# When an attention kernel starts its transposes, and when its planner counts results as ready

## The chip, the cores and the metric

The kernel runs on one core of a Trainium2 chip. The metric is the device time of one execution in microseconds (us). Three executions of the kernel before took 1045.03 us in the median, between 1043.71 and 1046.25 us. Engines are named as in the profile: PE is TensorE's matmul, PEld its weight load, DVE VectorE, ACT ScalarE, POOL GpSimd, SP the queue that issues the DMAs.

## The reference

Two attention blocks (A and B) with a compressive memory work on the same input of 2048 tokens and 640 channels, 32 heads of 20 channels, in four segments of 512 tokens. A gate that depends on the token mixes their results.

```python
logits = einsum("bhqd,bhkd->bhqk", qs, ks) * scale + mask   # mask: only earlier or equal keys
a_dot = einsum("bhqk,bhkd->bhqd", softmax(logits), vs)
a_mem = einsum("bhld,bhde->bhle", phi(qs), M) / (einsum("bhld,bhd->bhl", phi(qs), z)[..., None] + 1e-6)
o = g * a_mem + (1.0 - g) * a_dot          # g = sigmoid(beta), one value a head
M = M + einsum("bhld,bhle->bhde", phi(ks), vs); z = z + phi(ks).sum over tokens
...
out = gate * (o_A @ wo_A) + (1 - gate) * (o_B @ wo_B)    # gate = sigmoid((x * gate_w).sum(-1))
```

q, k and v are x @ wq, x @ wk, x @ wv; phi(t) is t + 1 above zero and exp(t) below.

## The kernel before

**Stages.** A pair of block and segment is called t (0 to 7), a group of four heads a quad, so that there are 64 quads, eight for each t. The large products (projections to q, k, v, and the output projection) are taken in three terms, of high and low parts of both factors, so that each has 15 or, for v, 60 matmuls on each half of the array. For a quad the kernel makes the scores once with queries on the partitions to find each row's maximum (an S unit, L1096; DVE reads the bank at L1114), and a second time with keys on the partitions (a T unit, L1186; ACT takes the exponential at L1209, POOL applies the causal mask at L1210). The probabilities then meet v in a block of 16 matmuls over the whole array (pv_unit, L1225 and L1237).

**Halves.** Except for the PV blocks and the first and the last products, a matmul uses 64 of the 128 rows of the array. The two halves are two lanes of work; a weight load for one half can pass while the other half streams. A product or a small unit has a part for each half: the first part writes the bank (`firsts`), the second, on the other half, adds to it later (`seconds`).

**Transposes.** A helper (`turn`, L839) transposes a 128-column block with a matmul against an identity of 64 x 64, four in each half for a unit. Units of this kind are: `back_unit` (phi(k) for the memory update, 30 of them), `fin_unit` (the result of a PV block, 64), `o_transpose` (the attention result for the output projection, 40), all at L843 in the profile, and `mrow_unit` (L1147, one transpose in each half at L1152, 64 units), which turns the row maxima of a quad into rows that T units need. Each waits in a list (`late`, filled by `later`, L625) until a lane has room.

**The order is planned.** Nothing is scheduled on the chip: while the program is built, a planner simulates the engines and writes down the order of each engine's instructions. It holds a cost for every operation (`put`, L201, with a duration in us), a time by which a result counts as ready after that (`DONE`, L159), the streaming time of a matmul (`mm`, L162), and the lead that a weight load takes (`FULL` 0.113 us, for a transpose `LEADT` 0.056 us). `op` (L264) places a matmul on a lane, `lane_step` (L1402) chooses what a lane does next: a score matmul that is due (`lane_ops`), else the second part of a unit, else the first part of one; `start_unit` (L1388) takes a unit from `late` before a new product. A product that is under way can be interrupted by a late unit of priority 0 alone, which is an `mrow_unit`. Every unit holds one of eight PSUM banks from its first matmul until its result has been read.

**The table.** `RULES` (L90) has a row for each of the 66 steps of the plan: the order of the quad's five S and five T units, and five numbers that say how the products are spread among them, how much DVE work may be outstanding, and how long after a first part a second one may follow. `rules` (L1495) reads it; a step without a row keeps the row before.

**Splitting q and k.** A finished q or k bank is read several times (`hi_lo_phi` L637, `hi_lo_out` L660): ACT copies the high part (L680), ACT takes an exponential or a relu from the same bank (L652, L657), DVE subtracts for the low part (L664), and two or one more DVE operations make phi (L647 and L648, or L654).

Of the kernel before, what the change touches and what calls it, by code (L numbers as in the profile page):

```python
# [42 lines left out]
def tile_gated_mix_infini_attn(  # L43
# [47 lines left out]
        0: "TTSTSTSTSS 1.055 2.80 0.30 8 0.0",  # L91
        1: "TSSTTSSTTS 1.010 2.38 0.33 4 0.0",
        2: "STTSTSSTST 1.010 1.93 0.39 8 0.0",
        3: "TSTSTSTSTS 0.978 2.38 0.24 8 0.0",
        4: "TSTSTSTSTS 1.010 2.38 0.30 8 0.0",
        5: "TSSTTSSTTS 1.010 2.38 0.30 8 0.0",
        6: "TSTSTSTSTS 0.931 2.38 0.30 6 0.0",
        7: "TTSTSTSTSS 1.031 2.38 0.30 8 0.0",
        8: "TSTSTSTSTS 1.009 2.38 0.30 8 0.9",
        9: "STSTSTSTST 0.982 2.95 0.37 8 0.0",  # L100
        10: "TSTSTSTSTS 1.044 2.38 0.30 8 0.0",
        11: "TTSSTTSSTS 1.010 2.92 0.32 8 0.0",
        12: "TSTSTSTSTS 0.935 2.22 0.35 6 3.4",
        13: "TSTSTSTSTS 1.010 2.67 0.30 8 1.6",
        14: "TSTSTSTSTS 1.010 2.38 0.30 8 0.0",
        15: "TSTSTSTSTS 1.022 1.56 0.26 8 0.0",
        16: "TSTSTSTSTS 0.947 2.38 0.30 8 0.0",
        17: "TSTSTSTSTS 1.056 2.38 0.30 8 0.0",
        18: "TSTSTSTSTS 0.946 2.38 0.31 8 0.0",
        19: "TSTSTSTSTS 0.954 2.38 0.30 8 0.0",  # L110
        20: "STTSTSSTST 1.010 2.38 0.39 8 0.0",
        21: "TSTSTSTSTS 1.005 2.81 0.30 8 0.0",
        22: "TSTSTSTSTS 1.048 1.51 0.36 8 0.0",
        23: "TSSTTSSTTS 1.025 2.74 0.30 8 0.0",
        24: "TSTSTSTSTS 0.968 3.16 0.30 8 3.5",
        25: "TSTTSSTSTS 1.010 1.69 0.22 8 0.0",
        26: "TSTSTSTSTS 1.010 2.38 0.30 8 0.0",
        27: "TSTSTSTSTS 1.055 1.45 0.32 8 0.0",
        28: "TSTSTSTSTS 0.927 2.38 0.22 4 0.0",
        29: "TTSTSTSTSS 1.010 3.28 0.30 8 0.0",  # L120
        30: "TSTSTSTSTS 0.905 2.38 0.35 8 0.3",
        31: "TSTSTSTSTS 1.022 2.38 0.23 8 0.0",
        32: "TSTSTSTSTS 0.939 3.80 0.26 8 0.0",
        33: "TSTSTSTSTS 1.048 2.75 0.30 8 0.0",
        34: "TSTSTSTSTS 0.901 2.38 0.38 8 0.0",
        35: "TSTSTSTSTS 0.973 2.38 0.30 6 0.0",
        36: "STTSTSSTST 1.010 2.38 0.36 8 0.0",
        37: "TSTSTSTSTS 1.003 2.38 0.30 6 0.0",
        38: "TSTSTSTSTS 1.052 2.38 0.34 6 0.0",
        39: "TSTSTSTSTS 0.989 2.38 0.30 8 0.0",  # L130
        40: "TSTSTSTSTS 1.010 2.49 0.30 4 2.5",
        41: "TSTSTSTSTS 1.056 2.70 0.30 8 0.0",
        42: "TSTSTSTSTS 1.010 2.38 0.25 4 0.0",
        43: "TTSTSTSTSS 0.989 2.67 0.30 8 0.0",
        44: "TSTSTSTSTS 1.047 3.23 0.38 8 0.0",
        45: "TSTSTSTSTS 0.929 2.38 0.30 8 0.0",
        46: "TSTSTSTSTS 1.010 2.38 0.30 8 0.0",
        47: "TSTSTSTSTS 0.990 2.38 0.39 8 0.0",
        48: "TSTSTSTSTS 1.006 2.38 0.30 4 0.0",
        49: "TSTSTSTSTS 1.052 2.38 0.30 6 0.0",  # L140
        50: "STSTSTSTST 1.010 3.53 0.30 8 0.0",
        51: "TSTSTSTSTS 1.010 3.63 0.23 8 1.2",
        52: "TSTSTSTSTS 1.010 2.38 0.30 8 0.0",
        53: "TSTSTSTSTS 1.032 2.38 0.30 8 0.0",
        54: "TSTSTSTSTS 1.026 2.53 0.30 8 3.7",
        55: "TSTSTSTSTS 1.010 2.38 0.36 4 0.0",
# [15 lines left out]
    def mm(n):  # L162
        return 0.008 + n * 0.0004333, FULL, 1
# [1238 lines left out]
    def lane_step(half):  # L1402
# [192 lines left out]
```

## Time and profile before

| | us |
|---|---|
| median of three executions | 1045.03 |
| the profiled execution, device time | 1042.96 |
| its span, from the first to the last instruction | 1041.3 |
| PE busy | 1031.3 |
| DVE, ACT, POOL busy | 760.8, 660.2, 581.7 |

The profile is of one execution. The span counts from the first to the last instruction; the device time has 1.66 us more around it. A busy PE only says that some half of the array has a matmul under way: each matmul's record also holds its way through the array, so that records of one half overlap. Two more things are needed to read the rows: in a timeline, neighbouring instructions of one kind are merged to one row with a count, whichever half they run on; and a weight load (PEld) that stands idle with a releaser behind it waited for that engine's result.

### The profile page before, as it was taken

The page shows a single profiled execution, that of the slowest core. Times are in us where ns is not written, and L with a number is a line of the kernel's source. Part 1 is how long each engine was busy: PE and PEld are TensorE (multiplying, and loading weights), DVE is VectorE, ACT ScalarE, POOL GpSimd, SP SyncE. Part 2 cuts the span into 40 slices and gives each one's busy share as a digit, 9 for nine tenths or more (in the row PEclk, how much of TensorE's full clock was granted, in tenths as well). Part 3 has the DMA queues.
Part 4 walks back from the last instruction along what each step waited for, and adds up shares of the span by engine and source line. Part 5 has one row for each costly group of instructions (what it writes and reads, how often), then busy time and mean ns, then how long its engine had stood idle before and what let it go on. Part 6 is the DMA issues. An engine that isn't in the chain of part 4 may idle for free.

```text
span 1041.3 us, 31917 instructions
## 1 busy us (share of the span) xinstructions
PE 1031.3 (99%) x11780; PEld 870.4 (84%) x11780; DVE 760.8 (73%) x2725; ACT 660.2 (63%) x1337; POOL 581.7 (56%) x1043
## 2 busy tenths in 40 slices
PE   9999999999999999999999999999999999999998
PEld 7987888888888878888798887988879888888776
DVE  4787877558776688775877768976577767978844
ACT  5476666667564685665756557576574746757572
POOL 3565654556454674747736457375773635736462
PEclk9999999999999999999999999999999999999999
DMA  8997677658575486755858458674576855858432
GB/s 269 295 302 187 205 214 215 191 161 269 136 251 157 137 291 187 226 177 151 262 146 255 134 153 279 202 244 136 163 226 204 266 152 182 264 148 242 117 117 76
DMA packets 110028, 207.97 MB, mean 200 GB/s; under 512 B 12464, under 2 KB 16560, under 8 KB 109872
## 3 DMA queue, kind: packets, MB, share of 16 engines
q1 hardware_dynamic: 109872, 205.93, 65.2%
q8 instruction: 93, 1.52, 0.6%
q14 instruction: 63, 0.52, 0.2%
HBM read 131.43 MB, written 73.40 MB: 197 GB/s over the span
## 4 chain that ended last, share of the span: by engine, by line
PE 89%; DVE 3%; DMA 3%; ACT 2%; issue 1%; POOL 1%; SPq 0%; ACTq 0%; DVEq 0%; POOLq 0%
PE bank L695 52%; PE bank L1237 13%; PE bank L1217 7%; PE bank L1127 7%; PE bank L843 4%; PE bank L883 3%; PE bank L805 2%; DVE bank L1114 1%; DMA kd<-row 1%; DMA wst<-in_x_dram 1%; PE bank L741 1%; PE bank L1152 0%; POOL wl L524 0%; DMA row<-in_xT_dram 0%; PE bank L1056 0%
## 5 line engine op out<-in xcount | busy, mean ns | idle before, releaser
L1114 DVE CUSTOM_DVE_ANT_0 bank<-bank,tri 128x384 f32<-128x384 f32 (+3 forms) x1024 | 474.0, 522 | 146.3 <-PE bank L1127 117.6
L695 PE MATMUL bank<-row,wh 64*128 64x512 f32 x2308 | 535.2, 407 | 0.0
L1209 ACT ACTIVATE p<-bank 128x512 f32<-128x512 f32 x606 | 333.3, 599 | 155.6 <-PE bank L1217 124.5
L1210 POOL TENSOR_SCALAR_AFFINE_SELECT p<-p 128x256 f32<-128x256 f32 (+1 forms) x606 | 218.7, 370 | 243.9 <-ACT p L1209 233.4
L695 PEld LDWEIGHTS bank<-row,wh 64*128 64x128 f32 x2308 | 325.9, 185 | 12.4 <-issue 2.6
L695 PE MATMUL bank<-row,wl 64*128 64x512 f32 x1154 | 302.5, 402 | 0.0
L524 POOL TENSOR_TENSOR wl<-wst,wh 128x640 fp32r<-128x640 f32 x115 | 179.6, 1566 | 74.7 <-ACT wh L522 73.1
L695 PE MATMUL bank<-wvh,row 64*128 64x320 f32 x1280 | 202.4, 317 | 0.1
L1127 PE MATMUL bank<-kst,qst 60*128 60x384 f32 (+3 forms) x1024 | 176.9, 321 | 0.9 <-DVE O L1304 0.4
L695 PEld LDWEIGHTS bank<-row,wl 64*128 64x128 f32 x1154 | 170.4, 186 | 4.8 <-issue 0.6
L1217 PE MATMUL bank<-qst,kst 62*128 62x384 f32 (+3 forms) x1024 | 172.8, 323 | 1.1 <-DVE mw L819 0.7
L695 PEld LDWEIGHTS bank<-wvh,row 64*128 64x128 f32 x1280 | 161.1, 185 | 2.9 <-issue 1.4
L1237 PE MATMUL bank<-p,vst 128*32 128x128 f32 (+2 forms) x1980 | 148.3, 430 | 0.0
L1114 DVE DVE_READ_ACCUMULATOR2_ANT mx<- 128x1 f32 x1024 | 146.7, 143 | 0.0
L1217 PEld LDWEIGHTS bank<-qst,kst 62*128 62x128 f32 x1024 | 125.3, 185 | 17.1 <-DVE mx L1114 4.6
L1127 PEld LDWEIGHTS bank<-kst,qst 60*128 60x128 f32 x1024 | 125.1, 185 | 13.0 <-DVE mx L1114 2.9
L1237 PEld LDWEIGHTS bank<-p,vst 128*32 128x32 f32 x1980 | 59.4, 109 | 87.6 <-issue 68.3
L695 PE MATMUL bank<-wvl,row 64*128 64x320 f32 x640 | 113.3, 312 | 0.0
L522 ACT CAST wh<-wst 128x640 fp32r<-128x640 f32 x119 | 86.5, 736 | 34.5 <-PE bank L695 27.6
L695 PEld LDWEIGHTS bank<-wvl,row 64*128 64x128 f32 x640 | 88.7, 185 | 0.7 <-issue 0.4
L499 POOL TENSOR_TENSOR wvl<-wst,wvh 128x640 fp32r<-128x640 f32 (+1 forms) x48 | 63.9, 1336 | 21.3 <-ACT wvh L496 21.0
L664 DVE TENSOR_TENSOR row<-bank,row 128x512 fp32r<-128x512 f32 x80 | 54.4, 688 | 29.1 <-ACT row L652 15.3
(100 smaller groups left out, 1224.1 us busy)
## 6 DMA issues: line engine op xcount, KB each, us to landing
qd<-row SPq DMA_DIRECT2D x120, 256.0 KB
kd<-row SPq DMA_DIRECT2D x120, 256.0 KB
qst<-qd SPq DMA_DIRECT2D x128, 240.0 KB
kst<-kd SPq DMA_DIRECT2D x128, 240.0 KB
wst<-in_a_wq_dram SPq DMA_DIRECT2D x20, 320.0 KB
wst<-in_a_wk_dram SPq DMA_DIRECT2D x20, 320.0 KB
wst<-in_b_wq_dram SPq DMA_DIRECT2D x20, 320.0 KB
wst<-in_b_wk_dram SPq DMA_DIRECT2D x20, 320.0 KB
```

What stands on the lines that cost most here:

```text
L499: put("G", 0.77 * n, lambda: nc.gpsimd.tensor_tensor(out=wl[:, a:b, :], in0=w3, in1=r32(wh[:, a:b, :]), op=ALU.subtract), end, prio=4)
L522: put("A", 0.625, lambda: nc.scalar.copy(wh, w3), lambda: put(lo_eng, lo_cost, lambda: lo.tensor_tensor(out=wl, in0=w3, in1=r32(wh), op=AL ...
L524: lambda: lo.tensor_tensor(out=wl, in0=w3, in1=r32(wh), op=ALU.subtract), end, prio=3), prio=6)
L664: put("D", 0.605, lambda: nc.vector.tensor_tensor(out=lo, in0=src, in1=r32(hi), op=ALU.subtract), out, prio=1)
L695: return nc.tensor.matmul(bank_of, lhsT=w[ROWS[half]], rhs=x_[ROWS[half]], start=start, stop=stop)
L843: return nc.tensor.transpose(px[:, n, r], block(n)[r], ident[r, r])
L1114: put("D", w / 960.0 + 0.085, lambda: nc.vector.tensor_tensor_reduce(out=sc[:, off:off + w], in0=sc[:, off:off + w], in1=tri[:, L - w:], s ...
L1127: lane_ops[half].append((mm(w), lambda pair=pair, qb=qb, off=off, w=w, r=r, sc=sc: nc.tensor.matmul(sc[:, off:off + w], lhsT=q[r, pair, P ...
L1209: put("A", 0.483, lambda: nc.scalar.activation(pt, sc, AF.Exp, scale=SCALE), lambda: (bank.give(sc), put("G", 0.15 + 0.105 * len(todo), la ...
L1210: "G", 0.15 + 0.105 * len(todo), lambda: nc.gpsimd.affine_select(out=blocks, in_=blocks, pattern=[[0, len(todo)], [1, P]], base=0, channel ...
L1217: lane_ops[half].append((mm(w), lambda pair=pair, kb=kb, off=off, w=w, r=r, sc=sc: nc.tensor.matmul(sc[:, off:off + w], lhsT=k[r, pair, P ...
L1237: nc.tensor.matmul(po[32 * j:32 * j + 32, P * kb:], lhsT=vst[t % 2][:, kb, h * E1:h * E1 + 32], rhs=pts[i, n, f][0][:, off:off + w], start ...
```

## The change

Five things change together; the arithmetic of the kernel stays as it is.

1. The planner's constants: a result counts as ready 0.27 us (ACT), 0.26 us (DVE) and 0.22 us (POOL) after the end of the operation in the plan, in place of 0.17, 0.135 and 0.11. A score maximum on DVE gets 0.02 us more and counts another 0.05 us later. A 512-column matmul streams 0.2323 us in the plan in place of 0.2298.
2. Transpose units (`turns`, the default of `later`) may start, in either part, right behind a matmul whose stream is shorter than the load of the next weights (`quick`), even ahead of score matmuls that are due and in the middle of a product. Elsewhere they may start only after they have waited for a time (`wait`) or where the lane has nothing else. Once a part has begun it runs to its end.
3. The rule by which an `mrow_unit` could break into a product is gone.
4. The low part of q and k is put on DVE's queue when both of ACT's reads of the bank are over, not when the first is.
5. The table has a sixth number, `wait`, and new rows; nine steps have none.

```diff
     RULES = {
-        0: "TTSTSTSTSS 1.055 2.80 0.30 8 0.0",
-        1: "TSSTTSSTTS 1.010 2.38 0.33 4 0.0",
...
+        0: "TSTSTSTSTS 0.969 2.38 0.27 8 0.0 1.6",
+        1: "TSTSTSTSTS 0.927 2.38 0.30 8 0.0 0.59",
+        2: "TSSTTSSTTS 1.020 2.38 0.36 8 0.0 1.90",
...
-    DONE = {"A": 0.17, "D": 0.135, "G": 0.11, "S": 0.0}
+    DONE = {"A": 0.27, "D": 0.26, "G": 0.22, "S": 0.0}
...
-        return 0.008 + n * 0.0004333, FULL, 1
+        return 0.008 + n * 0.000438, FULL, 1
...
         begun[half], lane[half] = start, start + stream
+        quick[half] = lead + 0.003 > stream
...
-    def later(prio, cost, ok, fn):
-        late.append((prio, next(seq), cost, ok, fn))
+    def later(prio, cost, ok, fn, turns=True):
+        late.append((prio, next(seq), clk[0] if turns else None, ok, fn))
...
             read = then_all(2, over)
-            hi_lo_out(pp, hi, lo, dst, m, read, then)
-            put("A", 0.483, lambda: nc.scalar.activation(r32(y), pp, AF.Exp), read, prio=1)
+            low = hi_lo_out(pp, hi, lo, dst, m, read, then, 2)
+            put("A", 0.487, lambda: nc.scalar.activation(r32(y), pp, AF.Exp), lambda: (low(), read()), prio=1)
...
-        put("A", 0.483, lambda: nc.scalar.copy(hi, src), low, prio=1)
+        low = then_all(reads, low_part)
+        put("A", 0.475, lambda: nc.scalar.copy(hi, src), low, prio=1)
+        return low
...
-                    put("D", w / 960.0 + 0.085, lambda: nc.vector.tensor_tensor_reduce(
+                    put("D", w / 960.0 + 0.105, lambda: nc.vector.tensor_tensor_reduce(
...
-                    ), then, prio=3)
+                    ), lambda: at(clk[0] + 0.05, then), prio=3)
...
-    def start_late(keep, upto=9):
+    def start_late(half, upto=9, only=False):
         for x in late:
-            prio, _, cost, ok, fn = x
+            prio, _, born, ok, fn = x
             if prio > upto:
                 return None
-            if len(bank.free) <= (0 if prio <= 0 else keep) or (prio > 2 and load["D"] > rule["calm"]):
+            if only and born is None or not only and born is not None and clk[0] - born < rule["wait"]:
+                continue
+            if not bank.free or (prio > 2 and load["D"] > rule["calm"]):
                 continue
...
     def lane_step(half):
+        begun_ = [u for u in seconds[half] if u["turn"] and len(u["ops"][half]) < u["n"][half]]
+        if begun_:
+            return run_second(half, begun_[0])
+        if firsts[half] and firsts[half][-1]["turn"]:
+            return run_first(half, firsts[half][-1])
+        if quick[half]:
+            for u in seconds[half]:
+                if u["turn"] and max(now[0], lane[half], begun[half] + 0.003 + LEADT) >= u["at"]:
+                    return run_second(half, u)
+            u = start_late(half, only=True)
+            if u:
+                firsts[half].append(u)
+                return run_first(half, u)
         if lane_ops[half]:
...
-        if len(firsts[half]) == 1 and firsts[half][0]["credit"] and len(firsts[half][0]["ops"][half]) > 2:
-            u = start_late(0, 0)
-            if u:
-                firsts[half].append(u)
...
```

`run_first` and `run_second` are new names for the code that emits one matmul of a unit's first or second part; it is otherwise as before.

More of the change, by code (lines that the diff above doesn't have):

```diff
@@ L1246, in pv_unit @@
         fetched[0] = now[0]
+        quick[:] = [True, True]
         def read():
@@ L1386, in start_late, with start_unit @@
                 return fn()
-    def start_unit(half):
-        u = start_late(0)
+    def start_unit(half, any_=False):
+        u = start_late(half)
         if u is None and not over[0]:
@@ L1496, in rules @@
         if i in RULES:
-            order, rule["span"], rule["calm"], rule["lag"], rule["room"], rule["hold"] = RULES[i].split()
+            order, rule["span"], rule["calm"], rule["lag"], rule["room"], rule["hold"], rule["wait"] = RULES[i].split()
             rule.update({x: float(rule[x]) for x in rule if x != "order"}, order=order)
```

135 lines of the change are left out of this document (40 added, 95 removed), and 54 rows, old and new, of the table RULES.

## The prediction

> **What bounds the kernel now.** The page comes first: the span, the busy times, the granted clock and the shares of the chain that ended last.
>
> ```profile
> span 1041.3 us, 31917 instructions
> PE 1031.3 (99%) x11780; PEld 870.4 (84%) x11780; DVE 760.8 (73%) x2725; ACT 660.2 (63%) x1337; POOL 581.7 (56%) x1043
> ...
> PEclk9999999999999999999999999999999999999999
> ...
> PE 89%; DVE 3%; DMA 3%; ACT 2%; issue 1%; POOL 1%; SPq 0%; ACTq 0%; DVEq 0%; POOLq 0%
> ```
>
> The chain lies on PE for 89%, at the full clock in every slice, and no other engine passes 73%. So the time is the sum of what PE does on its two halves, plus what it loses between matmuls. I look for two kinds of loss: weight loads that don't fit behind a short matmul, and weight loads that wait for another engine. Next come the groups that the change moves, each shape apart.
>
> ```profile
> L1217 PEld LDWEIGHTS bank<-qst,kst 62*128 62x128 f32 x1024 | 125.3, 185 | 17.1 <-DVE mx L1114 4.6 <-DVE row L648 2.4 <-DVE mw L819 1.2
> ...
> L843 PE MATMUL bank<-ident,row 64*128 64x64 f32 x752 | 74.5, 225 | 0.0
> ...
> L843 PEld LDWEIGHTS bank<-ident,row 64*128 64x128 f32 x752 | 64.2, 138 | 3.1 <-DVE mx L1114 0.3 <-issue 0.2 <-PE bank L843 0.2
> ...
> L843 PE MATMUL bank<-ident,O 64*128 64x64 f32 x320 | 35.8, 225 | 0.1
> ...
> L1217 PE MATMUL bank<-qst,kst 62*128 62x128 f32 x256 | 43.3, 221 | 0.0
> L1127 PE MATMUL bank<-kst,qst 60*128 60x128 f32 x256 | 43.2, 220 | 0.0
> ...
> L1152 PE MATMUL bank<-ident,mt 64*32 64x64 f32 x128 | 27.9, 218 | 0.0
> ```
>
> There are 752 + 320 + 128 = 1200 transposes and 512 score matmuls of 128 columns. A transpose's load of 128 columns is recorded with 138 ns, that of a score matmul with 185 ns: by their own records transposes load faster.
>
> **The price of a short matmul.** A timeline of PE around 473 us has one half on a steady product, while the other does something else.
>
> ```profile
> 472.99 0.39 PE L695 MATMUL bank<-row,wl 64*128 64x512 f32 x1
> ...
> 473.22 0.40 PE L695 MATMUL bank<-row,wh 64*128 64x512 f32 x1
> ...
> 473.45 0.39 PE L695 MATMUL bank<-row,wh 64*128 64x512 f32 x1
> ...
> 473.69 0.39 PE L695 MATMUL bank<-row,wl 64*128 64x512 f32 x1
> ```
>
> Three intervals take 0.70 us: 0.233 us a 512-column product. Now a place at 804 us where both halves end a short matmul at the same moment, and one goes on with a product, the other with four transposes.
>
> ```profile
> 804.34 0.40 PE L1127 MATMUL bank<-kst,qst 60*128 60x384 f32 x4
> 804.58 0.44 PE L695 MATMUL bank<-row,wh 64*128 64x512 f32 x1
> 804.58 0.41 PE L843 MATMUL bank<-ident,O 64*128 64x64 f32 x4
> 804.80 0.48 PE L695 MATMUL bank<-row,wh 64*128 64x512 f32 x2
> ```
>
> The first row ends at 804.74 (two 384-column matmuls and, last, the two of 128). The product behind it ends at 804.58 + 0.44 = 805.02, 0.28 us later: 0.05 more than the steady 0.233, because its weights weren't in yet. The transposes end at 804.99, 0.25 us for four, 0.0625 each, and nothing is lost ahead of them. The product behind them ends at 805.28, 0.29 us later: behind a transpose, too, 0.05 to 0.06 are lost. So a run of n transposes costs a half 0.0625 n + 0.05 wherever it stands, and right behind a 128-column matmul it takes away the 0.05 that this would have lost by itself.
>
> **The order: 3.7 us less.** I counted the runs of transposes, half by half, in the instruction orders of the two built programs. Matmuls are the same in number and shape (10,252), and so are DVE's, ACT's, POOL's and SP's operations, but for five PSUM copies that go from ACT to DVE. The runs are 348 before and 313 after; 33 of them stand behind a 128-column matmul before and 127 after, 37 behind a PV block before and 58 after. Ninety-four more runs that use a short matmul's gap: 94 x 0.05 = 4.7. Thirty-five runs that have grown together with another: 35 x 0.05 = 1.75. Twenty-one more behind a PV block, which like a short matmul ends with no weights loaded: 21 x 0.05 = 1.05. That is 7.5 us of one half's time; two halves share it: 3.7 us. The bounds: nothing, if the other half is always the later one where they meet at a PV block, and 7.5, if it is always this one.
>
> In sentences by themselves: the Trainium skill, page "TensorE: Matmul & The Clock Gate", section "LDWEIGHTS (loading the stationary operand)", says that a load takes its columns divided by 1.2 in ns whatever the number of rows. A transpose with 128 columns would then load for 107 ns like any other and would gain nothing behind a short matmul; the 3.7 would shrink to the 0.9 of the merged runs. The trace disagrees: four transposes in 0.25 us have no room for 107 ns each.
>
> **The waits: 5 us less.** Around 474 us PE waits for a score maximum.
>
> ```profile
> 473.64 0.69 DVE L1114 CUSTOM_DVE_ANT_0 bank<-bank,tri 128x512 f32<-128x512 f32 x1
> 474.25 0.14 DVE L1114 DVE_READ_ACCUMULATOR2_ANT mx<- 128x1 f32 x1
> ...
> 474.44 0.19 PEld L1217 LDWEIGHTS bank<-qst,kst 62*128 62x128 f32 x2 [0.51 <-DVE mx L1114]
> ...
> 474.44 0.50 PE L1217 MATMUL bank<-qst,kst 62*128 62x512 f32 x2
> ```
>
> The operation starts at 473.64, its last part ends at 474.39 (0.75 us), and the load begins 0.05 later. The pair of 512-column matmuls takes 0.50 where a single one has 0.39 above, so about 0.1 passes until the array streams: 0.75 + 0.05 + 0.1 = 0.90 us from DVE's start. The plan before counts 0.618 + 0.135 = 0.75 (512/960 + 0.085, and DONE), the plan after 0.638 + 0.05 + 0.26 = 0.95. For ACT:
>
> ```profile
> L1209 ACT ACTIVATE p<-bank 128x512 f32<-128x512 f32 x606 | 333.3, 599 | 155.6 <-PE bank L1217 124.5
> ```
>
> 0.60 + 0.05 + 0.1 = 0.75; the plan before has 0.483 + 0.17 = 0.65, after 0.75. So the new constants lie behind the bare result, as the change says, but they are close to when PE can use it. The plan before puts a matmul that needs a bank 0.10 (ACT) to 0.15 us (DVE) too early, and on an engine that takes its instructions in order everything behind it waits too. How much is lost shows in the view of waits.
>
> ```profile
> PEld bank L1217 <- DVE mx L1114: 4.6, 20, 0.5
> PEld bank L1127 <- DVE mx L1114: 2.9, 12, 0.5
> PEld bank L1217 <- DVE row L648: 2.4, 8, 0.4
> ...
> PEld bank L805 <- ACT row L859: 0.8, 2, 0.4
> ...
> PEld bank L1237 <- ACT wh L522: 0.2, 1, 0.2
> ```
>
> These are the first and the last of 29 rows in which PE's weight loads wait for DVE or ACT (three of the start left out): 22 us in 79 waits, 0.28 us each. Taking 0.13 off each gives 79 x 0.13 = 10 us. I take half, 5 us, because an instruction put later lets another go first that has waits of its own: counted in the built orders, and with the intervals above, the time from the matmul that fills a bank to the one that uses it again hardly grows (by DVE's maximum 1.98 us at the lower quartile before, 2.02 after; by ACT's exponential 1.43 and 1.41). The bounds: 22 us, all of it, and a loss, priced with the rivals below.
>
> The low part of q and k belongs here:
>
> ```profile
> DVE row L664 <- ACT row L652: 15.3, 20, 1.9
> DVE row L664 <- ACT row L657: 8.7, 8, 5.6
> ```
>
> DVE stood 24 us with this operation at its head, waiting for ACT's second read; queued behind it were score maxima, and PE waited for those. Put later, it lets them pass. With DVE at 73% this is worth only what PE waits for it, so it is a part of the 22 and gets no term; the cover gone, it would cost at most these 24.
>
> **The end: nothing.** With no products left, a later start would show in full.
>
> ```profile
> 1026.30 2.19 PE bank L695 x18
> ...
> 1029.21 4.34 PE bank L1056 x18
> 1033.57 3.44 DVE row L1041 x5
> ```
>
> In the chain before, 2.19 us of products stand between the last `fin_unit` and the last `o_transpose`, then 30 whole-array products, of which 15 need that transpose, and five DVE additions close it. In the order after, 17 half products and 8 of the whole-array ones stand in the first gap, more cover than before, and 7 in the second. By the chain's 4.34 / 18 = 0.24, seven give 1.7 us, against ACT's 0.6 and DVE's 0.69 (the copies of L1332 are shaped like L1209 and L1114): covered, with at most 0.3 lost.
>
> The sum: 3.7 + 5 = 8.7 us off the profiled execution's 1042.96, which is 1034.3. That execution was 2.07 us below the median of the three runs; against the median the forecast is 1045.03 - 8.7 = 1036.3 us.
>
> **Rivals.**
>
> *The order alone.* The waits move rather than shrink: after as before some 22 us of weight loads wait. For it speak the unchanged times of reuse; against it the plan's error of 0.10 to 0.15 us, which the rows show. 1045.0 - 3.7 = 1041.3 us.
>
> *All waits gone.* Each listed wait is 0.28 us long in the mean, twice the shift, so this asks that waits come from one another. 1045.0 - 3.7 - 22 = 1019 us.
>
> *Banks held too long: slower.* A transpose unit takes its bank with its first part, and its second part now looks for a short matmul on the other half. With the intervals above, the built orders have 1.15 us from the first to the last transpose of a unit before and 1.52 after (134 units of eight), and 0.71 and 1.35 (64 units of two): 134 x 0.37 + 64 x 0.64 = 91 us of one bank. If all eight banks are wanted at every moment, this costs 91 / 8 = 11 us, with the 5 us of the waits not gained: 1045.0 - 3.7 + 11 = 1052 us. It decides once waits for banks (L1114, L1209) pass what they are now by some 4 us. Against it: 91 us is 1.1% of eight banks over 1041 us, and products need few of them.
>
> *No shorter load.* If a transpose's load held up a half as long as a product's, only the merged runs and the waits would count: 1045.0 - 0.9 - 5 = 1039 us. This is the skill's rule from above; the row with 0.25 us for four speaks against it.
>
> *Nothing to measure.* What the order gives is lost to waits at new places: 1045 us.
>
> **How the numbers follow.** About 0.2%, 2.1 us, is what a measurement of this kernel tells from no change. The forecast has a chance of 0.46, the order alone 0.16, all waits gone 0.10, banks held 0.18, no shorter load 0.02, nothing 0.08. Faster by over 0.2% are the first three and the load: 0.74; within 0.2%: 0.08; slower: 0.18. The forecast's own range is 1028 to 1041. For 8 in 10 it goes down to 1023, short of the case with all waits gone, and up to 1050, short of the full price of the held banks.
>
> **What would show it.** Right: in the profile after, PE's loads wait for DVE and ACT less than 22 us, by about 5 to 10; L664's successor no longer waits for ACT's second read; the transposes' records count and last as before. Wrong for the order: products behind short matmuls still end 0.28 us after them, at the places where transposes now stand. Wrong for the waits: the rows of DVE's maximum or of ACT's exponential grow. A lower granted clock, or DMA waits ahead of S units, would be causes that I have left out.

## The result and the profile after

The changed kernel takes 1027.15 us in the median of four executions (1026.22 to 1028.6), beside 1044.37 us for the kernel before on the same chip (1042.63 to 1046.25). The ratio is 0.9836, its 95% interval 0.9813 to 0.9859: 17 us less, about twice the forecast. That is below the forecast's own range of 1028 to 1041 us and inside its range for 8 in 10, 1023 to 1050. The profiled execution took 1026.22 us, against 1042.96 before.

The page of the kernel after, the same rows as before: span, busy times, granted clock, and the shares of the chain that ended last.

```profile
span 1024.5 us, 31917 instructions
...
PE 1015.8 (99%) x11780; PEld 873.7 (85%) x11780; DVE 760.0 (74%) x2725; ACT 659.3 (64%) x1337; POOL 581.5 (57%) x1043
...
PEclk9999999999999999999999999999999999999999
...
PE 95%; DMA 2%; DVE 1%; ACT 1%; POOL 0%; issue 0%; SPq 0%; ACTq 0%; DVEq 0%
```

The instructions are the same in number, and the busy times of DVE, ACT and POOL are the same to 1 us; PE's falls by 15.5 us with the span, and PEld's grows by 3.3. The chain that ends last now lies on PE for 95% in place of 89%: DVE had 3% of it and has 1%, ACT 2% and has 1%, POOL 1% and has none. So the program waits less for the other engines.

Where in the program the time went shows in a table by stretches: after each stretch and its length come the busy time and instruction count of PE, PEld, DVE, ACT and POOL, then the granted clock, the DMA share and GB/s. First the kernel before, then the one after.

```profile
0.00:130.00 130.00, 127.52 (x1332) 108.26 (x1334) 93.54 (x331) 81.28 (x165) 69.44 (x126) 1.00 0.82 251
130.00:520.00 390.00, 388.43 (x4520) 330.29 (x4517) 287.73 (x1027) 254.49 (x517) 225.37 (x398) 1.00 0.67 202
520.00:900.00 380.00, 379.18 (x4408) 321.84 (x4409) 283.14 (x1022) 240.31 (x484) 218.17 (x386) 1.00 0.65 198
```

```profile
0.00:130.00 130.00, 127.67 (x1367) 110.74 (x1369) 91.27 (x313) 79.15 (x160) 67.94 (x118) 1.00 0.86 265
130.00:520.00 390.00, 389.49 (x4634) 337.75 (x4632) 298.57 (x1078) 264.61 (x536) 230.92 (x412) 1.00 0.68 202
520.00:900.00 380.00, 379.04 (x4470) 329.11 (x4468) 286.18 (x1032) 240.57 (x489) 222.64 (x393) 1.00 0.67 203
```

PE is busy 98 to 100% of each stretch in both, and yet it gets through 35, 114 and 62 more matmuls after. "Busy" means that at least one half streams; what has gone must be time in which the other half stood still, and the count of intervals below finds it. It went nearly everywhere, not at one place.

**Where the transposes stand.** A timeline of PE in the kernel after, at a place like the one at 804 us in the prediction; the columns are start, duration, engine, line, operation and tiles.

```profile
241.69 0.22 PE L1122 MATMUL bank<-kst,qst 60*128 60x128 f32 x1
241.75 0.22 PE L838 MATMUL bank<-ident,row 64*128 64x64 f32 x1
...
241.82 0.34 PE L838 MATMUL bank<-ident,row 64*128 64x64 f32 x3
241.97 0.47 PE L690 MATMUL bank<-row,wl 64*128 64x512 f32 x1
```

The 128-column score matmul ends at 241.91. Four transposes, now at L838, end at 241.82 + 0.34 = 242.16, 0.25 us later, and the product behind them at 241.97 + 0.47 = 242.44, 0.28 after that. These are the 0.0625 each, and the 0.05 lost once, that the prediction read from the kernel before.

**What PE's loads wait for.** The largest waits of PE's weight loads for DVE's maximum and ACT's exponential, after (us in all, times, longest).

```profile
PEld bank L1122 <- DVE mx L1109: 1.3, 5, 0.4
...
PEld bank L1232 <- DVE mx L1109: 1.2, 3, 0.5
PEld bank L838 <- ACT row L1204: 1.1, 1, 1.1
PEld bank L1122 <- ACT p L1204: 1.0, 3, 0.6
...
PEld bank L1212 <- DVE mx L1109: 1.0, 4, 0.3
```

L1122, L1212 and L1109 are the old L1127, L1217 and L1114. The two score rows for the maximum have fallen from 4.6 and 2.9 us to 1.0 and 1.3. Over all rows for DVE and ACT, counted as in the prediction: 21.9 us in 79 waits before, 12.8 in 38 after. DVE's part fell from 17.7 to 6.0; ACT's rose from 4.2 to 6.8.

The low part of q and k, in the view of DVE's waits (L657 is the old L664; L645 and L650, the old L652 and L657, are the exponential and the relu, one of which is ACT's second read of a bank):

```profile
DVE row L657 <- ACT row L650: 14.8, 12, 5.6
...
DVE row L657 <- ACT row L645: 3.5, 5, 1.3
```

DVE waits for that read 18.3 us in place of 24.0. Where it is the exponential, 3.5 in place of 15.3 (37 banks after, 42 before); where it is the relu, 14.8 in place of 8.7 (23 and 18).

**Order and waits apart.** I took each half's intervals from the end of one matmul to the end of the next (a PV block counts as one), and for every pair of shapes the median interval over both traces. The sum of the medians is what an order costs when nothing is late; the rest is excess, the time of waits as far as a half really stood still for them, whether or not the other half's work hid it in the view of waits. The mean of the two halves, in us, from the first matmul's end to the last one's:

| | order | excess | together |
|---|---|---|---|
| before | 992.0 | 42.0 | 1034.0 |
| after | 988.2 | 29.4 | 1017.6 |
| difference | -3.8 | -12.6 | -16.4 |

How far shapes are told apart moves this split a little: grouped more finely or more coarsely, the order falls by 3.1 to 4.1 us and the excess by the rest of the 16.4.

By the widths of two neighbours, most of the excess that went lies in five pairs: 512 columns behind 512 went from 9.1 to 5.9 us, 512 behind 320 from 3.5 to 1.1, 384 and 256 behind 512 from 2.9 to 0.8 and from 2.4 to 0.7, 384 behind 320 from 3.2 to 1.9. A width of 512 can be a product's or a score matmul's. With the two kept apart, product behind product hardly changes (512 columns each, 6.0 to 5.3), and a score matmul of 512 columns behind a product goes from 3.1 to 0.9. Summed by what comes next, the excess ahead of score matmuls goes from 18.2 to 6.3 us, ahead of products from 12.7 to 13.7, ahead of transposes from 5.6 to 4.6. So nearly all that went stood ahead of score matmuls. One that stands right behind a product begins a unit, and so needs a bank.

**The end**, in the chain of the kernel after:

```profile
1009.61 2.15 PE bank L690 x17
1011.76 2.05 PE bank L1051 x8
1013.81 0.40 PE bank L838 x4
1014.22 0.04 issue
1014.26 0.46 PE bank L838 x4
1014.72 2.51 PE bank L1051 x10
1017.23 0.02 issue
1017.25 3.44 DVE row L1036 x5
```

The last transposes come right behind the 17 half products and 8 whole-array ones that the prediction named as their cover; no wait stands between them but two gaps of 0.04 and 0.02 us, and DVE's last additions take 3.44 us as before.

### The profile page after: what moved, and what is told of

The parts are those of the page before. It is cut to its first block, busy times and chain, and to the rows that moved or that the text cites. A ratio compares the mean times of both kernels' runs of the same rounds, so it can differ in the third digit from the quotient of the medians.

```text
span 1024.5 us, 31917 instructions
## 1 busy us (share of the span) xinstructions
PE 1015.8 (99%) x11780; PEld 873.7 (85%) x11780; DVE 760.0 (74%) x2725; ACT 659.3 (64%) x1337; POOL 581.5 (57%) x1043
## 4 chain that ended last, share of the span: by engine, by line
PE 95%; DMA 2%; DVE 1%; ACT 1%; POOL 0%; issue 0%; SPq 0%; ACTq 0%; DVEq 0%
PE bank L690 54%; PE bank L1232 13%; PE bank L1122 7%; PE bank L1212 7%; PE bank L838 4%; PE bank L800 3%; PE bank L878 3%; DMA qd<-row 2%; PE bank L1147 1%; PE bank L736 1%; PE bank L328 1%; DMA wst<-in_a_wo_dram 1%; PE bank L1051 0%; DVE bank L1109 0%; DVE row L1036 0%
## 5 line engine op out<-in xcount | busy, mean ns | idle before, releaser
L1109 DVE CUSTOM_DVE_ANT_0 bank<-bank,tri 128x256 f32<-128x256 f32 (+3 forms) x1024 | 475.2, 519 | 135.3 <-PE bank L1122 107.6
L690 PE MATMUL bank<-row,wh 64*128 64x512 f32 x2308 | 528.3, 404 | 0.0
L1204 ACT ACTIVATE p<-bank 128x512 f32<-128x512 f32 x596 | 328.7, 601 | 142.0 <-PE bank L1212 110.1
L690 PEld LDWEIGHTS bank<-row,wh 64*128 64x128 f32 x2308 | 330.0, 186 | 8.9 <-issue 0.6
L690 PE MATMUL bank<-row,wl 64*128 64x512 f32 x1154 | 308.7, 399 | 0.0
L690 PE MATMUL bank<-wvh,row 64*128 64x320 f32 x1280 | 198.4, 316 | 0.1
L690 PEld LDWEIGHTS bank<-row,wl 64*128 64x128 f32 x1154 | 180.3, 186 | 4.4
L1122 PE MATMUL bank<-kst,qst 60*128 60x384 f32 (+3 forms) x1024 | 176.8, 318 | 1.3 <-ACT row L1259 0.6
L1212 PE MATMUL bank<-qst,kst 62*128 62x384 f32 (+3 forms) x1024 | 173.1, 318 | 0.2 <-ACT row L854 0.2
L1232 PE MATMUL bank<-p,vst 128*32 128x512 f32 (+3 forms) x1952 | 148.3, 429 | 0.0
L1109 DVE DVE_READ_ACCUMULATOR2_ANT mx<- 128x1 f32 x1024 | 144.2, 141 | 0.0
L1122 PEld LDWEIGHTS bank<-kst,qst 60*128 60x128 f32 x1024 | 131.1, 185 | 8.6 <-DVE mx L1109 1.3
L1212 PEld LDWEIGHTS bank<-qst,kst 62*128 62x128 f32 x1024 | 128.9, 186 | 6.8 <-DVE mx L1109 1.0
L838 PE MATMUL bank<-ident,row 64*128 64x64 f32 x752 | 72.7, 225 | 0.8 <-ACT row L1204 0.8
```

The costliest lines, as they stand in the source:

```text
L690: return nc.tensor.matmul(bank_of, lhsT=w[ROWS[half]], rhs=x_[ROWS[half]], start=start, stop=stop)
L838: return nc.tensor.transpose(px[:, n, r], block(n)[r], ident[r, r])
L1109: put("D", w / 960.0 + 0.105, lambda: nc.vector.tensor_tensor_reduce(out=sc[:, off:off + w], in0=sc[:, off:off + w], in1=tri[:, L - w:], s ...
L1122: lane_ops[half].append((mm(w), lambda pair=pair, qb=qb, off=off, w=w, r=r, sc=sc: nc.tensor.matmul(sc[:, off:off + w], lhsT=q[r, pair, P ...
L1204: put("A", 0.483, lambda: nc.scalar.activation(pt, sc, AF.Exp, scale=SCALE), lambda: (bank.give(sc), put("G", 0.15 + 0.105 * len(todo), la ...
L1212: lane_ops[half].append((mm(w), lambda pair=pair, kb=kb, off=off, w=w, r=r, sc=sc: nc.tensor.matmul(sc[:, off:off + w], lhsT=k[r, pair, P ...
```

## The experiments

In the tables, "ratio" is the time divided by that of the kernel before, run beside it. "Plan" is the time at which the planner itself, at build, holds its last instruction to be over; "span" is that of the profiled execution. The two ends are not the same event: behind the last matmul the plan has 1.3 to 1.4 us, the chip 4.4 to 5.4. Order and excess are as above, with the same medians. "For DVE" is the wait of PE's weight loads for DVE, the start included.

### The constants and the table crossed

Either kernel with the three constants of the other (point 1 of the change); the tables stay. Against the kernel after, for `a_olddone` (`b_newdone` is the opposite edit in the kernel before):

```diff
-    DONE = {"A": 0.27, "D": 0.26, "G": 0.22, "S": 0.0}
+    DONE = {"A": 0.17, "D": 0.135, "G": 0.11, "S": 0.0}
...
-        return 0.008 + n * 0.000438, FULL, 1
+        return 0.008 + n * 0.0004333, FULL, 1
...
-                    put("D", w / 960.0 + 0.105, lambda: nc.vector.tensor_tensor_reduce(
+                    put("D", w / 960.0 + 0.085, lambda: nc.vector.tensor_tensor_reduce(
...
-                    ), lambda: at(clk[0] + 0.05, then), prio=3)
+                    ), then, prio=3)
```

> The kernel before with the new constants alone (ready times, streaming time, cost of the score maximum); transposes, low part and table as before. By counted order it should gain nothing from transposes (46 of 345 runs behind a short matmul). Theory 'constants': the waits fall by 8 to 12 us without any other part, so about 1034 us. Rival 'table': the gain came with the rows searched anew, so about 1044 us or slower, since the old rows do not fit. Rival 'low part': 1044 us.

> The changed kernel with the old constants; transposes, low part and table as changed. By counted order it keeps the gain of the transposes (113 of 341 runs behind a short matmul). Theory 'constants': the waits come back, 8 to 12 us, so about 1037 us. Rivals 'table' and 'low part': 1027 to 1030 us.

| | median us | ratio | plan | span | order + excess | for DVE |
|---|---|---|---|---|---|---|
| before | 1044.37 | 1 | 1014.2 | 1041.3 | 992.0 + 42.0 | 19.6 |
| b_newdone | 1064.42 | 1.0196 (1.0179 to 1.0213) | 1056.0 | 1063.3 | 993.1 + 63.4 | 14.5 |
| a_olddone | 1063.36 | 1.0192 (1.0177 to 1.0207) | 1031.9 | 1060.3 | 988.8 + 64.8 | 15.9 |
| after | 1027.15 | 0.9836 (0.9813 to 0.9859) | 1023.5 | 1024.5 | 988.2 + 29.4 | 7.9 |

By the ratios both are 20 us slower than the kernel before. New constants alone do not bring the gain, and new code with its table loses 37 us without them. Only the rival 'table' of `b_newdone` (1044 us or slower) had room for this; 1063 us for `a_olddone` is outside all that was expected. The page of `b_newdone` shows what kind of time it is:

```profile
span 1063.3 us, 31871 instructions
...
PE 87%; DMA 6%; DVE 3%; ACT 2%; POOL 1%; issue 1%; SPq 1%; ACTq 0%; DVEq 0%; POOLq 0%
```

Loads wait 5 us less for DVE, and yet the chain has left PE more often. The new constants put every later instruction elsewhere, and the old rows no longer suit what comes out: the plan itself has become longer, 1056 us. The order part hardly moves with the constants (992.0 to 993.1, 988.2 to 988.8): that part belongs to the code. Beside this, one column tells something new. With old constants the span is 27 and 28 us longer than the plan, with new ones 7 and 1. The last matmul alone tells the same: in the kernel before it ends 23 us later on the chip than in the plan, in the kernel after 2 us earlier. The plan before was wrong about the chip, the plan after is nearly right.

### No table

Both kernels with one row for all steps (`b_flat`; in `a_flat` it has a sixth number, 1.6):

```diff
-        0: "TTSTSTSTSS 1.055 2.80 0.30 8 0.0",
...
+        0: "TSTSTSTSTS 1.010 2.38 0.30 8 0.0",
```

> The kernel before with one row of the table for all steps, TSTSTSTSTS 1.010 2.38 0.30 8 0.0, in place of 66. Theory 'constants': the old rows were chosen by a plan that is too early, so they are worth little: 1040 to 1050 us. Rival 'table': the rows are worth 10 us or more: 1055 us.

> The changed kernel with one row for all steps, the same as in the flat kernel before, and wait 1.6. Theory 'constants': 1028 to 1034 us, because the new rows are worth little. Rival 'table': 1037 us or more, 10 us being the rows' part.

| | median us | ratio | plan | span | order + excess | for DVE |
|---|---|---|---|---|---|---|
| b_flat | 1076.34 | 1.0315 (1.0295 to 1.0335) | 1047.9 | 1075.1 | 993.3 + 75.0 | 15.7 |
| a_flat | 1077.48 | 1.0328 (1.0306 to 1.035) | 1068.2 | 1078.9 | 988.9 + 82.7 | 7.7 |

Without a fitted table the code and its constants gain nothing: the order part falls by 4.4 us as ever, the waits for DVE halve, and the excess takes it all back. (In `a_flat` 8 us of it are a halved clock, in `b_flat` 3; see the last section.) By the ratios a table is worth 33 us to the old kernel and 51 to the new one, two to three times the whole change. So the tables have to be put on one footing before the code can be judged.

### The same short search for each combination

From a flat row, 8000 random changes of one to three numbers of the table, each kept if the plan did not end later; the same for all four.

```diff
-        0: "TSTSTSTSTS 1.010 2.38 0.30 8 0.0",
+        0: ..., 65: ...
```

> The code before, with a table searched afresh from the flat one by 8000 random changes of rows, each kept when the planner's own end came no later. The planner's end is 1021.7 us (flat 1047.9; the table before 1014.2). In the six traces so far a plan with the old constants is 26 to 28 us shorter than the chip's span. Theory 'fit' (the plan and how far its table is searched set the time): span 1047 to 1051 us, device time about 1050. Rival 'rows are tuned on more than the plan': a table that only shortens the plan gives little, 1065 us or more.

> The code before with the new constants, table searched by the same 8000 changes. The planner's end is 1035.4 us; plans with the new constants were 1 to 11 us shorter than the span. Theory 'constants' (with true ready times an equal search ends lower on the chip): 1037 to 1046 us, below the fit of the old constants. Rival 'fit alone': within 4 us of it, 1047 to 1053 us.

> The changed code (transposes behind short matmuls, later low part) with the old constants, table searched by the same 8000 changes. The planner's end is 1020.0 us, the counted order is 4.7 us shorter than that of the code before. Theory 'fit': plan + 27 = 1047, device time about 1048 us. Theory 'transposes' (their 4 us arrive whatever the table): 4 to 5 us below the fit of the code before.

> The changed code and constants, table searched by the same 8000 changes. The planner's end is 1041.9 us, where the table of the change has 1023.5. Theory 'fit': 1044 to 1053 us, so 17 us or more above the changed kernel, whose advantage is then its longer searched table. Theory 'constants and transposes': both gains add, so 1035 us or less.

| | median us | ratio | plan | span | order + excess | for DVE |
|---|---|---|---|---|---|---|
| b_fit: old code, old constants | 1052.46 | 1.0082 (1.0065 to 1.0099) | 1021.7 | 1049.6 | 992.5 + 50.3 | 19.9 |
| b_newdone_fit: old, new | 1043.22 | 0.9991 (0.9981 to 1.0002) | 1035.4 | 1042.3 | 993.2 + 42.3 | 10.5 |
| a_olddone_fit: new, old | 1045.36 | 1.0012 (1.0 to 1.0023) | 1020.0 | 1044.0 | 987.7 + 48.6 | 12.2 |
| a_fit: new, new | 1044.06 | 0.9998 (0.9989 to 1.0008) | 1041.9 | 1042.0 | 989.5 + 45.6 | 6.1 |

In the old code the new constants give 9 us, and the waits of PE's loads show it. First `b_fit`, then `b_newdone_fit`, the rows for DVE's maximum of the three lines with most:

```profile
PEld bank L1217 <- DVE mx L1114: 3.6, 11, 0.8
...
PEld bank L1127 <- DVE mx L1114: 3.3, 13, 0.4
...
PEld bank L1237 <- DVE mx L1114: 3.2, 10, 0.4
```

```profile
PEld bank L1237 <- DVE mx L1114: 2.1, 7, 0.4
...
PEld bank L1127 <- DVE mx L1114: 1.4, 6, 0.3
...
PEld bank L1217 <- DVE mx L1114: 0.8, 4, 0.2
```

34 waits with 10.1 us have become 17 with 4.3. The new code gives 7 us with old constants, 5 of them in the order. But both together were no better than either alone. The plan of `a_fit` ended at 1041.9, and the span was 0.1 us longer: the chip kept the plan, and the search, which here began with a `wait` of 1.6, had ended at a poor table. A search of this length doesn't settle it.

### A long search

About 32,000 to 37,000 further changes for each combination. `a_deep` began anew with a `wait` of 0.5; none of its rows is from the change. The first of them:

```diff
-        0: "TSTSTSTSTS 0.969 2.38 0.27 8 0.0 1.6",
-        1: "TSTSTSTSTS 0.927 2.38 0.30 8 0.0 0.59",
...
+        0: "TSTSTSTSTS 0.925 2.98 0.31 8 0.0 0.51",
+        1: "TSTSTSTSTS 0.926 3.30 0.32 4 2.4 0.50",
```

In `a_noquick_deep`, searched alike with a `wait` of 0, the rule for short matmuls never applies; the low part and the unbroken runs stay:

```diff
-        quick[half] = lead + 0.003 > stream
+        quick[half] = False
...
-        quick[:] = [True, True]
+        quick[:] = [False, False]
```

> The code before with the new constants, its table searched by 36,800 further changes after the first 8000. The planner's end is 1031.0 us, 4.4 below that of the shorter search. Theory 'true constants let the search reach the chip': the 4.4 us arrive, span about 1032 to 1038, device time 1034 to 1039 us, that is 5 to 10 us below the kernel before without any transpose behind a short matmul; the rest of the changed kernel's gain is then the 4 to 5 us of the order and its table. Rival 'search gains in the plan only': 1043 us as the shorter search.

> The changed code with the old constants, its table searched by 35,000 further changes. The planner's end is 1019.0 us, only 1.0 below that of the shorter search. Theory 'the plan and its offset of 24 to 28 us set the time': span 1043 to 1047, device time about 1045 us, so that transposes alone, with their 4 us in the order, stay no faster than the kernel before; the old constants cap it. Rival 'transposes': below 1035 us.

> The changed code and constants with a table of my own search: 8000 and again 31,600 random changes from a flat table with wait 0.5, without any row of the change's table. The planner's end is 1028.2 us (the change's table: 1023.5); counted order 988.4 us a half. Theory 'both parts together let a search go low' (constants keep the plan true, transposes behind short matmuls take 3 us of order): 1030 to 1036 us, 5 us or more below the code before with the new constants (1040.2). Rival 'only the rows of the change's table are good': 1040 us or more.

> The changed code and constants without the rule for short matmuls (the flag quick is never set, wait 0), so that 32 of 278 runs of transposes stand behind one; table searched by 8000 and 32,000 changes. The planner's end is 1033.3 us, counted order 990.6. Theory 'both parts': 1035 to 1041 us, that is 3 to 6 us above the same search with the rule, about the difference of the orders (2.2) and of the plans (5.1). Rival 'the rule is worth nothing once the table is fitted': as with the rule, within 2 us.

> The code and constants before, table searched by 8000 and 33,800 changes. The planner's end is 1019.6 us, 2.1 below the shorter search, whose kernel took 1052.5 us. Theory 'a plan that is too early wastes the search': 1047 to 1051 us, at the plan's 28 us of offset, so 10 us or more above the same search with the new constants. Rival 'a longer search alone would have done': 1040 us or less.

| | median us | ratio | plan | span | order + excess | for DVE |
|---|---|---|---|---|---|---|
| b_deep: old code, old constants | 1053.57 | 1.0078 (1.0054 to 1.0102) | 1019.6 | 1052.4 | 992.5 + 53.2 | 19.9 |
| b_newdone_deep: old, new | 1040.2 | 0.9963 (0.9949 to 0.9977) | 1031.0 | 1043.7 | 992.6 + 43.6 | 8.8 |
| a_olddone_deep: new, old | 1045.39 | 1.0013 (1.0004 to 1.0023) | 1019.0 | 1045.1 | 987.7 + 50.7 | 14.4 |
| a_noquick_deep: new without the rule, new | 1039.34 | 0.9951 (0.9934 to 0.9968) | 1033.3 | 1039.0 | 992.5 + 39.7 | 6.2 |
| a_deep: new, new | 1032.1 | 0.988 (0.9861 to 0.9898) | 1028.2 | 1031.3 | 989.7 + 34.7 | 10.1 |

(The profiled execution of `b_newdone_deep` took 1045.4 us, 5 more than its other five; its span and its split are too long by that much. The clock was halved in it for 6.8 us, from 574.7 us on, which is 3.4 of the 5.)

Of what was expected, `b_newdone_deep` came out at 1040.2, between its theory (1034 to 1039) and its rival (1043), and `b_deep` 3 us above its theory.

Now the four corners add up. In points, hundredths of the ratio, the new constants give 1.0078 - 0.9963 = 1.15 in the old code and 1.0013 - 0.988 = 1.33 in the new: 12 and 14 us. The new code gives 0.65 with old constants and 0.83 with new ones: 7 and 9 us. Of the latter the rule for short matmuls is 0.9951 - 0.988 = 0.71, or 7 us; the low part and the unbroken runs, 0.9963 - 0.9951 = 0.12, are within the scatter. The rule's 7 us are 2.8 of order (992.5 to 989.7) and 5.0 of excess (39.7 to 34.7). The page of `a_deep`:

```profile
span 1031.3 us, 31858 instructions
...
PE 95%; DMA 2%; ACT 1%; DVE 1%; POOL 1%; issue 1%; ACTq 0%; DVEq 0%
```

It has the chain of the kernel after, with a table that has nothing to do with the change's. With old constants more search no longer reached the chip: from `b_fit` to `b_deep` the plan fell by 2.1 us and the time didn't, and from `a_olddone_fit` to `a_olddone_deep` by 1.0 to no effect. These steps are no larger than the intervals of the times, so they show that the search had little left to find, not what a larger step would have done.

### How much hangs on one row, and on which half of the program

`a_row2` changes one number of the kernel after, the time after which a second part may follow in step 2. `a_half` keeps its rows up to step 32 and is flat from there.

```diff
-        2: "TSSTTSSTTS 1.020 2.38 0.36 8 0.0 1.90",
+        2: "TSSTTSSTTS 1.020 2.38 0.28 8 0.0 1.90",
```

```diff
-        33: ..., 65: ...
+        33: "TSTSTSTSTS 1.010 2.38 0.30 8 0.0 1.6",
```

> The changed kernel with one number of one row altered: how long after a first part a second may follow, 0.28 in place of 0.36 us, in step 2 of 66. Everything else of the code, constants and the other rows stays; the count of transposes behind short matmuls is nearly the same (110 for 127). The planner's end goes from 1023.5 to 1048.4 us. Theory 'fit' (rows are fitted to the exact order that the earlier rows make): 1049 to 1058 us. Rival 'constants and transposes carry the gain': within 3 us of 1027.

> The changed kernel with its rows for steps 0 to 32, then one flat row for steps 33 to 65. The planner's end is 1042.5 us. Theory 'fit': the first half runs as in the changed kernel, to within 1 us at the thirty-third block of probabilities times v, and the loss of 19 us or more comes after it. Rival 'rows are worth little where the constants are true': within 5 us of 1027.

| | median us | ratio | plan | span | order + excess | for DVE |
|---|---|---|---|---|---|---|
| a_row2 | 1054.59 | 1.010 (1.008 to 1.012) | 1048.4 | 1051.8 | 989.7 + 55.3 | 12.4 |
| a_half | 1054.16 | 1.0078 (1.005 to 1.0106) | 1042.5 | 1052.4 | 988.9 + 56.7 | 9.9 |

One number costs 27 us, more than the change gives. The plan knew it (1023.5 to 1048.4). In `a_half` the 33rd PV block starts 496.3 us after the first, in the kernel after 494.2: 2 us later, where 1 was expected. From there to the last matmul it takes 490.8 us, the kernel after 466.2; of these 25 us some 7 are the halved clock of the last section. So a bad table costs its time where it holds, and a good beginning is not lost later. The flat second half also leaves work for the end that should have been done by then, as the rows from 1000 us on show (columns as above):

```profile
1000.00:1025.00 25.00, 24.41 (x222) 16.05 (x223) 14.06 (x54) 18.05 (x38) 16.46 (x36) 0.86 0.24 79
1025.00:1053.00 28.00, 21.39 (x175) 15.81 (x165) 9.94 (x19) 5.30 (x10) 2.44 (x6) 0.89 0.14 48
```

In the same kernel no product runs on PE from 1001.4 to 1017.5 us, so none hides what the units wait for, and the chain leaves PE from 1001.17 to 1010.20:

```profile
1001.17 0.73 ACT wh L491
...
1002.97 0.99 ACT p L1180 x2
1003.96 0.62 ACT wh L491
1004.65 1.56 POOL wl L493
1006.46 1.53 POOL wvl L493
1008.23 1.08 POOL p L1181 x3
```

## Why the prediction was right and where it was wrong

**The order: right.** Forecast 3.7 us less, found 3.8 (3.1 to 4.1, by how shapes are grouped). The places measured after the change have the four numbers of the prediction: 0.25 us for four transposes, 0.28 to the end of the next product. The order part is 987.7 to 989.7 us in every kernel that has the rule and 992.0 to 993.3 in every one that lacks it, whatever the table. That two halves share it is built into this count and not shown by it.

**The waits: the step that failed.** The prediction had two numbers, 79 waits by 0.13 = 10 us, and went on: "I take half, 5 us, because an instruction put later lets another go first that has waits of its own". The excess fell by 12.6 us, the listed waits alone by 9.1. The mechanism was right: 11.9 us of excess went ahead of the score matmuls. This part of the excess also tells old constants from new in the other runs. It is 18.0 to 22.8 us in all seven kernels with old constants; with new ones it is 6.3 to 15.9 us in nine of the ten, and 23.9 in `a_flat`, whose clock was halved for a while. In the equal searches the constants take it from 18.6 to 11.5 and from 22.8 to 7.8 in the old code, from 18.0 to 10.1 and from 20.1 to 7.0 in the new. The size was less than half of what came, for two reasons.

First, the halving was a guess, and the argument behind it, that the times of reuse hardly grow, looked at the wrong thing. What fell is not the length of a wait, which rose from 0.28 to 0.34 us in the mean, but their number, from 79 to 38: with other matmuls in front, half of them no longer arise. Over the seven kernels with old constants PE's loads wait 16.8 us for DVE in the mean (12.2 to 19.9), over the ten with new ones 9.4 (6.1 to 14.5).

Second, the other half of the worth lies in what the constants do to the table. In a plan that runs 24 to 33 us ahead of the chip, which the seven kernels with old constants show, a row that shortens the plan need not shorten the time. With new constants the two differ by 0 to 13 us over ten kernels, and by 1.0 in the kernel after. Taken at the last matmul, and without the time that halved clocks cost, the chip is 20 to 30 us behind the plan with old constants, 4 to 6 with new ones in the old code, and within 3 us of it with new ones in the new code. The table, which the prediction took for part of the order and gave no term, decides whether the gain is there: with the old one the same constants cost 20 us. Part of this could be known before the result: the planner's own end comes out of the building of the program, and before it was 1014.2 us, 27.1 short of a span of 1041.3. The prediction compared single waits with the plan, and not its end.

What was also not priced is that transposes behind short matmuls may save waits beside their 0.05 us: with the rule 5 us of excess go in the searched pair, more than its order part. No run separates why, nor this from the scatter of the search.

**How the sum closes.** By equal long searches, constants and code together give 1.0078 - 0.988 = 1.98 points, 20.7 us. The table before is 0.78 points better than what my search found for that kernel, the change's table 0.44 better than what it found for the new one: 1.98 - 0.78 + 0.44 = 1.64 points, the measured 17 us. All these are ratios to the same kernel, so this sum closes whatever the cause; it only says how much each table counts for. Against the forecast's 1034.3 for the profiled execution it took 8.1 less: 7.6 from the waits, 0.1 from the order, and 0.4 lie outside the intervals counted.

**The waits' own signs.** PE's loads were to wait "about 5 to 10" us less: 9.1. The rows of DVE's maximum fell, from 8.7 to 3.7 us in all. ACT's didn't, although its constant moved by 0.10: those of the exponential grew from 1.6 to 2.5 us, which the prediction had named as a sign against the waits. The growth is small beside DVE's fall, but no gain by ACT's constant shows. Over all kernels PE's loads wait 7.8 us for ACT in the mean with old constants and 9.2 with new ones.

**The low part: half wrong.** "L664's successor no longer waits for ACT's second read" holds for most of the exponentials, 15.3 to 3.5 us, and not for the relus, whose wait grew from 8.7 to 14.8 us with five more of them. Giving it no term was right: low part and unbroken runs together are 0.12 points.

**The end: right.** The forecast was nothing, with 17 and 8 products as cover, and the chain has them and two gaps of 0.06 us in all.

**The rivals.** The order alone (1041) and nothing to measure (1045) fall with the time, and so does the missing short load (1039), by its own place too: four transposes in 0.25 us. All waits gone (1019) asked for 22 us; 12.8 are still there. Banks held longer was to decide once waits for banks grow by some 4 us; in the kernel after those for DVE's maximum fell by 5 us and those for ACT's exponential grew by 1. But slower outcomes were as near as that chance made them, and by another mechanism: the same code with rows that don't suit it is 10 (`a_row2`) to 34 us (`a_flat`) slower than before.

**What stays open.** The three constants were only run together. The streaming time is a part of the plan's error too: half of the array streams some 1.53 million columns of products and scores, and the constant grows by 0.0000047 us a column, which by estimate makes about 7 of the plan's 27 us. The low part was not run alone. Each combination was searched once, at most twice, and two searches for the same code, begun with another `wait`, ended 12 us apart on the chip (`a_fit`, `a_deep`), though not after equally many changes; the shares of 13 and 8 us for constants and code have that uncertainty, while their signs agree in both pairs. Whether a longer search reaches the change's table was not tried; none of these kernels beats it.

## What to carry to other kernels

Where a program's order comes from a plan, compare the plan's own end with the measured span first: 27 us of difference were a sign that the plan was wrong about when results are ready and how long matmuls stream, and the search for good parameters could only follow it. A corrected cost isn't judged with the old parameters, nor new parameters with the old cost, since each table fits one exact order; cross them, and then fit all corners with the same effort. Don't halve a count of waits without a row that says why: ask whether each wait would be shorter, or would not arise.

## What was not expected of the hardware

In `a_half` the granted clock is 0.86 and 0.89 in the two stretches after 1000 us quoted above. In shorter stretches it shows as two values, 1.00 and 0.50 (columns as above):

```profile
1005.70:1009.10 3.40, 3.23 (x30) 2.47 (x28) 3.26 (x15) 3.29 (x8) 3.40 (x7) 1.00 0.06 8
1009.10:1015.90 6.80, 6.59 (x39) 3.03 (x39) 4.52 (x20) 2.90 (x7) 2.90 (x8) 0.50 0.12 37
...
1036.40:1039.80 3.40, 1.93 (x14) 1.15 (x13) 2.10 (x6) 0.62 (x2) 0.00 (x0) 1.00 0.00 0
1039.80:1043.20 3.40, 3.40 (x9) 2.63 (x10) 0.69 (x1) 0.52 (x1) 0.00 (x0) 0.50 0.00 0
```

So here PE thins out first, at full clock (busy 3.23 and 1.93 of 3.40 us), and the halved clock follows. It costs time: in the chain a PV block at half clock takes 4.15 us, a later one 2.29.

```profile
1012.17 4.15 PE bank L1208 x32
...
1023.37 2.29 PE bank L1208 x32
```

With another 3.4 us from 695.1 us on, `a_half` loses some 7 us in this way (reckoned as half the length of such stretches). Before their last matmul five of the 17 profiled executions have such stretches, ten in all, each 3.4 or 6.8 us long: `a_flat` loses 8 us by them, `b_flat` and `b_newdone_deep` 3, `a_row2` 2. Ahead of nine of the ten, PE stood idle for 0.2 to 1.8 us of the 3.4 us before. An idle stretch alone does not bring it: `b_newdone_fit` and `a_deep` have some with 1.7 us and keep the full clock. So waits can cost more than their own length; what decides it stays open.

The kernel before and the one after have no such stretch while PE works. In the latter the clock is halved only behind the last matmul, which ends at 1020.0 us, and nothing is lost by it:

```profile
1000.00:1020.00 20.00, 19.90 (x179) 15.04 (x169) 10.26 (x22) 5.50 (x10) 3.14 (x7) 1.00 0.06 23
1020.00:1022.80 2.80, 0.00 (x0) 0.00 (x0) 0.69 (x1) 0.00 (x0) 0.00 (x0) 0.99 0.92 311
1022.80:1024.50 1.70, 0.00 (x0) 0.00 (x0) 0.00 (x0) 0.00 (x0) 0.00 (x0) 0.50 0.00 1
```
